# Spreading VectorE's row statistics over the block groups, and ending the DMA transposes two groups early

## The chip, the cores and the metric

The kernel runs on one core of one Trainium2 chip. The metric is device time in microseconds (us) of one execution.

## The reference, cut to what matters

```python
x = A_x                                              # 2048 tokens x 1024, bf16
x = x + _A_ref(_layernorm(x), A_w_r, A_w_i)          # spectral filter: rfft2, times W, irfft2
x = x + _B_ref(_layernorm(x), B_w1, B_b1, B_w2)      # dense 1024 -> 3584, mish, dense 3584 -> 1024
x = x + _A_ref(_layernorm(x), A_w_r, A_w_i)
x = x + _B_ref(_layernorm(x), B_w1, B_b1, B_w2)
```

The change concerns the two dense layers `_B_ref` with their layer normalisation; the same program text makes both. "First layer" and "second layer" below mean these two.

## The kernel before

Tokens are held as 16 tiles of 128, four to a chunk. A dense layer multiplies chunks 0 and 1 with the first weights, the last eight of its fourteen weight blocks as *block groups* (`quads`); then come 16 half-tile products with the second weights for these chunks (`mm2`, "the second product"); then the same for chunks 2 and 3, there with all fourteen blocks as groups. While chunks 0 and 1 are multiplied, tiles 8 to 15 must be normalised by VectorE and transposed by DMAs for their own turn. That work hangs on the groups through the function `after`.

A block group saves a product by working with sums of weight blocks and sums of tokens. Its seven products of four matmuls land in three PSUM banks (PSUM, `PS` in the profile's rows, holds the results of the matmuls), and VectorE's five additions (`add`) tie them together:

```python
for n in range(N + 1):
    if n < N:
        product(n, a, "A11", "B11", True); ...copy by ScalarE...
        product(n, b, "S2", "T2", True);   add(u2, b, p1)
    if n:                                   # the group before is finished here
        product(n - 1, pb, "A22", "T4", False); add(q1, pb, q1); ...
        product(n - 1, pd, "S4", "B22", False); add(q2, pd, q2); ...
        after(n - 1)                        # <- statistics, roots, normalisations, transposes
    if n < N:
        ...three more products...
        add(u3, b, p1); add(u3, d, u3)      # the next A22 and S4 add to these banks
```

VectorE runs its program in order, so whatever `after` puts in delays the two `u3` additions, and TensorE (PE) waits for these before its next `A22`.

```python
def stats_half(self, j, h): ... bn_stats ...        # stats_dve(j): two of these and a bn_aggr
def scales(self, j0, n):                            # the "root chain": 1/sqrt by 8 tiny steps for n tiles
    on(tensor_scalar ...); on(tensor_scalar ... int32 ...)
    for _ in range(2):
        on(tensor_tensor(a, r, r, mult)); on(tensor_tensor(a, a, h, mult)); on(scalar_tensor_tensor ...)
def apply(self, j, out=False): ... tensor_scalar(b, XS[j], mean, r, subtract, mult)   # the normalisation
def turned(c, t, xn): ... eight closures, each one SyncE DMA with transpose=True, appended to `turning`
def turn(n): ... pops n of them into SyncE's program
def normal(j): ... apply(j), then turned(...)
def residual(j): ... XS[j] += spectral part, by VectorE
def token_sums(p, last): ... three, then one more, subtractions of transposed tiles for the next groups
```

SyncE also issues the loads of the second weights (`load_w2`). The second product begins with 20 matmuls on weight blocks loaded earlier; the first two blocks (`load_w2(0, 0)` and `(0, 1)`) share memory with the slot of the last group and can be loaded only when PE has finished that group. In the first layer GpSimd forms the weight sums (`fill_slot`: one addition and three subtractions for each of the groups' blocks, called its subtractions below) beside all this and keeps them in DRAM; in the second layer they are only loaded.

## Time and profile before

| | before |
|---|---|
| time, median of the first 3 runs | 1009.95 us (1009.22 to 1011.17) |
| span of the profiled run | 1006.9 us |
| busy: PE, VectorE, ScalarE, GpSimd | 92%, 51%, 38%, 16% |
| first layer: eight groups, then 16 second products | 59.66 us, 104.76 us |
| second layer: the same | 53.31 us, 99.85 us |
| all the rest | 689.32 us |

The stretches are read from PE's rows in order of time: from the first matmul of the groups to the first of the second product, and from there to the next block product. At PE's pace the groups need 48.4 us and the 448 matmuls of a second product 96.8 us; what a stretch has beyond that is waiting or a slow clock. The lines that carry this stand in the prediction.

In the lines of the profile, L1188 are the groups' matmuls, L1193 their additions, L1241 the matmuls of the second product, L1253 its additions, L1164 the token sums, L1084 GpSimd's subtractions, L499 to L512 the root chain, L521 the normalisation, L250 and L251 the DMAs; x84 means 84 instructions merged into one row. A granted clock of 1.00 is PE's full speed.

### The profile page before, as it was taken

What the parts mean: (1) busy time and instruction counts of PE and PEld (TensorE: products, weight loads), DVE (VectorE), ACT (ScalarE), POOL (GpSimd) and SP (SyncE); (2) the same over time, 40 slices, a digit from 0 to 9 for tenths busy, and PEclk for the clock granted to TensorE, in tenths of its full rate; (3) what the DMA queues carried; (4) which work ended last, traced back from release to release, by engine and by line L of the source; (5) the groups of instructions that cost most, each with busy time, mean ns of one, the idle gap of its engine ahead of it and who ended that gap; (6) DMA issues with size and microseconds to landing.
All of it is one profiled execution on the core that took longest, in us unless ns stands there. A gap on an engine that the chain in (4) does not pass through costs nothing. (4 is left out here: it accounts for less than half of the span.)

```text
span 1006.9 us, 13694 instructions
## 1 busy us (share of the span) xinstructions
PE 928.8 (92%) x5650; PEld 490.6 (49%) x5650; DVE 513.1 (51%) x947; ACT 377.9 (38%) x531; POOL 158.7 (16%) x184
## 2 busy tenths in 40 slices
PE   0899699897999999999998987998899999999998
PEld 0677475343444444444447756743344444444443
DVE  6697567785227655525326855748611325551111
ACT  7798484352000255500008966644400015550000
POOL 3831007910600050000621200000000000000000
PEclk9999899898999999999999997999999999999999
DMA  9969844545611164220941885344281114421000
GB/s 276 274 202 324 204 117 149 211 145 178 212 34 50 53 225 146 95 89 32 225 98 43 236 219 147 147 146 123 88 249 22 58 37 161 164 94 63 32 32 21
DMA packets 140431, 136.48 MB, mean 136 GB/s; under 512 B 74368, under 2 KB 121296, under 8 KB 140368
## 3 DMA queue, kind: packets, MB, share of 16 engines
q1 hardware_dynamic: 127264, 95.26, 31.9%
q0 software_dynamic: 10928, 38.69, 11.8%
q10 hardware_dynamic: 2176, 1.66, 0.5%
q8 instruction: 44, 0.72, 0.3%
q14 instruction: 19, 0.16, 0.0%
HBM read 97.49 MB, written 33.55 MB: 130 GB/s over the span
## 5 line engine op out<-in xcount | busy, mean ns | idle before, releaser
L1241 PE MATMUL PS<-ARENA 128*128 128x512 bf16 x1792 | 389.9, 380 | 8.7 <-DMA ARENA<-in_B_w_dram 8.7
L1188 PE MATMUL PS<-ARENA 128*128 128x512 f16 (+1 forms) x1232 | 271.7, 382 | 14.6 <-DVE ARENA L1193 14.1
L1241 PEld LDWEIGHTS PS<-ARENA 128*128 128x128 bf16 x1792 | 175.6, 98 | 222.6 <-issue 12.6
L1188 PEld LDWEIGHTS PS<-ARENA 128*128 128x128 bf16 x1232 | 120.0, 98 | 165.7 <-DVE ARENA L1193 21.6
L1193 DVE TENSOR_TENSOR ARENA<-PS,ARENA 128x512 f32<-128x512 f32 x220 | 151.1, 691 | 93.9 <-PE PS L1188 91.9
L1253 DVE TENSOR_TENSOR XS<-PS,XS 128x512 bf16<-128x512 f32 x63 | 43.6, 692 | 276.2 <-PE PS L1241 276.2
L577 ACT ACTIVATE ARENA<-PS 128x512 f32<-128x512 f32 (+2 forms) x66 | 51.8, 784 | 257.3 <-PE PS L1188 246.9
L1198 ACT ACTIVATE ARENA<-ARENA,B 128x512 bf16<-128x512 f32 x132 | 95.2, 722 | 73.3 <-DVE ARENA L1193 67.7
L1084 POOL TENSOR_TENSOR ARENA<-ARENA 128x512 bf16<-128x512 bf16 x56 | 68.3, 1219 | 124.6 <-DVE ARENA L521 59.3
L1149 PE MATMUL PS<-ARENA 128*128 128x256 bf16 (+1 forms) x576 | 87.5, 310 | 0.3
L1149 PEld LDWEIGHTS PS<-ARENA 128*128 128x128 bf16 x576 | 55.8, 99 | 27.1 <-DVE ARENA L1115 1.0
L469 DVE BATCH_NORM_STATS2 BN<-XS 128x6 f32<-128x512 bf16 x99 | 64.2, 678 | 6.2 <-DMA XS<-in_A_x_dram 5.2
L1153 ACT ACTIVATE ARENA<-PS,B 128x256 bf16<-128x256 f32 (+1 forms) x72 | 38.4, 542 | 36.0 <-PE PS L1149 35.4
L1198 ACT ACTIVATE ARENA<-PS,B 128x512 bf16<-128x512 f32 x44 | 30.3, 688 | 20.4 <-PE PS L1188 20.4
L441 ACT ACTIVATE RS<-MV,EPS 128x2 f32<-128x2 f32 (+2 forms) x5 | 1.5, 297 | 95.6 <-DVE MV L472 83.7
L802 PE MATMUL PS<-ARENA 128*128 128x256 bf16 x256 | 32.4, 273 | 3.9 <-DVE ARENA L791 3.2
L780 ACT ACTIVATE ARENA<-PS 128x1024 bf16<-128x1024 f32 x32 | 33.3, 1071 | 4.5 <-PE PS L776 4.5
L728 PE MATMUL PS<-FD,ARENA 128*128 128x256 bf16 (+1 forms) x256 | 31.8, 271 | 2.9 <-DVE ARENA L995 1.6
L784 DVE TENSOR_TENSOR ARENA<-ARENA 128x1024 bf16<-128x1024 bf16 x32 | 22.0, 688 | 20.9 <-ACT ARENA L780 15.3
L1164 DVE TENSOR_TENSOR ARENA<-ARENA 128x2048 f16<-128x2048 bf16 x16 | 22.7, 1417 | 17.7 <-PE PS L1149 17.3
L813 ACT ACTIVATE ARENA<-PS 128x1024 bf16<-128x1024 f32 x28 | 29.9, 1090 | 3.8 <-PE PS L802 3.8
L1023 PE MATMUL PS<-MT,ARENA 128*128 128x32 bf16 (+1 forms) x512 | 21.5, 201 | 10.2 <-DMA ARENA<-u_scratch 6.8
(95 smaller groups left out, 705.3 us busy)
## 6 DMA issues: line engine op xcount, KB each, us to landing
ARENA<-in_B_w_dram SPq DMA_DIRECT2D x62, 512.0 KB, 5.8
ARENA<-w1s_scratch SPq DMA_DIRECT2D x30, 896.0 KB, 4.6
w1s_scratch<-ARENA POOLq DMA_DIRECT2D x14, 896.0 KB, 4.0
u_scratch<-ARENA SPq DMA_DIRECT2D x14, 512.0 KB, 3.8
ARENA<-u_scratch SPq DMA_DIRECT2D x14, 512.0 KB, 5.8
w_scratch<-ARENA POOLq DMA_DIRECT2D x8, 512.0 KB, 7.2
ARENA<-w_scratch POOLq DMA_DIRECT2D x8, 512.0 KB, 5.3
out_dram<-XS SPq DMA_DIRECT2D x16, 256.0 KB, 2.0
```

The lines of the kernel that those rows point to most:

```text
L469: self.op(self.dve, lambda e: e.bn_stats(self.BN[:, j, 6 * h:6 * h + 6], self.XS[:, j, 512 * h:512 * h + 512]), reads=[self.r_xs[j]], part ...
L577: fn = (lambda e: e.activation(dst, src, ACT.Copy)) if scale is None else \
L780: self.op(act, lambda e: e.activation(x.ap.rearrange("p a b -> p (a b)"), ps, ACT.Copy, scale=SIG), reads=banks, writes=[x.res])
L802: fns.append(lambda e, c=c, part=part: e.matmul(ps[:, c * 256:(c + 1) * 256], yk.ap[:, part, c * P:(c + 1) * P], t[:, (128, 0)[part]:(384, ...
L1084: self.op(self.pool, lambda e, dst=A(dst), x=A(x), y=A(y), op=op: e.tensor_tensor(dst, x, y, op), reads=[b.res] + list(after), writes=[b.rs])
L1149: fns.append(lambda e, db=db, bank=bank, fl=fl: e.matmul(PS[:, bank, 0:w], wb.ap[:, db, fl * P:(fl + 1) * P], x.ap[:, db, tok], start=(db ...
L1153: self.op(act, lambda e, bank=bank, ft=ft: e.activation(at.ap[:, ft, tok], PS[:, bank, 0:w], ACT.Mish, bias=self.B1[:, ft:ft + 1]), reads= ...
L1188: self.group([lambda e, db=db: e.matmul(PS[:, bank, :], A[:, db, :], mov[:, db, :], start=(start and db == 0), stop=(db == 3), skip_group_ ...
L1193: self.op(dve, lambda e: e.tensor_tensor(dst.ap, PS[:, bank, :], x.ap, ALU.add), reads=[self.r_bank[bank], x.res], writes=[dst.res])
L1198: self.op(act, lambda e: e.activation(at.ap[:, ft, :], src, ACT.Mish, bias=self.B1[:, ft:ft + 1]), reads=[res, self.r_b1], writes=[ra])
L1241: fns.append(lambda e, ft=ft, w=W2[h][ft // 4]: e.matmul(PS[:, bank, :], at.ap[:, ft, t * P:(t + 1) * P], w.ap[:, ft % 4, :], start=(ft == ...
L1253: self.op(dve, lambda e: e.tensor_tensor(xs, PS[:, bank, :], xs, ALU.add), reads=[self.r_bank[bank]], writes=[self.r_xs[j]])
```

## The change

The intent: at most one statistic or one root chain of two tiles in a block group, beside at most one normalisation, so that VectorE comes back in time for its additions; and no transposes in SyncE's queue in the last two groups, so that the weight loads go out at once. What no longer fits goes into the loop of the second product.

```diff
--- before.py
+++ after.py
@@ -1390,18 +1390,17 @@
             if 1 <= n < 4:
                 for i in ((2,), (3, 4), (5, 6))[n - 1]:
                     load_w2(0, i)
-            for j in ((8, 9), (), (10,), (11,), (), (12,), (13,), ())[n]:
+            for j in ((8,), (9,), (), (10,), (11,), (), (), ())[n]:
                 self.stats_dve(j)
-            if n == 0:
-                self.scales(8, 2)
-            if n == 3:
-                self.scales(10, 2)
-            if 1 <= n < 5:
-                normal(7 + n)
-            if n in (2, 3):
-                for j in range(8 + 2 * n, 10 + 2 * n):
+            if n in (2, 5):
+                self.scales(8 + 2 * (n // 4), 2)
+            if n in (2, 3, 5, 6):
+                normal((0, 0, 8, 9, 0, 10, 11)[n])
+            if n > 5:
+                for j in range(2 * n, 2 * n + 2):
                     residual(j)
-            turn(4)
+            if n < 6:
+                turn(4)
         quads(list(range(6, 14)), order, B, after)
         for i in range(2):
             load_w2(0, i)
@@ -1413,14 +1412,18 @@
         self.xn_buf = [self.alloc(f"XN{i}", self.ob["TS"] + i * 2048, [self.D]) for i in range(4)]
         for n in range(16):
             if n == 0:
+                self.stats_dve(12)
+                self.stats_dve(13)
+                self.scales(12, 2)
+            if n == 1:
                 self.stats_dve(14)
                 self.stats_dve(15)
-                self.scales(12, 4)
+                self.scales(14, 2)
             if n < 4:
                 normal(12 + n)
             t = n % 8
             mm2(t // 4, t % 4, n // 8)
-            turn(4)
+            turn(5)
             if n == 10:
                 token_sums(1, last=False)
                 B = token_sums(1)
```

## The prediction

> **What bounds the kernel now.** The page gives the frame: TensorE (PE) is busy 92% of the span and ends the chain, so the change can gain only what PE waits. I read PE's waits next, longest first.
>
> ```profile
> PE PS L598 <- DVE ARENA L595: 21.8, 1, 21.8
> PE PS L1188 <- DVE ARENA L1193: 14.1, 9, 4.9
> PE PS L1241 <- DMA ARENA<-in_B_w_dram: 8.7, 2, 5.7
> ```
>
> The columns are total us, times, longest. The first is in the prologue, which the diff leaves alone. The second is PE in the first dense product (block products, L1188) waiting for VectorE's additions; the third is PE at the start of the second product (L1241) waiting for weights. The changed code runs in both dense layers, so I read PE in order of time there, the first layer above, the second below.
>
> ```profile
> 174.38 12.25 PE L1188 MATMUL PS<-ARENA 128*128 128x512 bf16 x56
> 191.54 21.52 PE L1188 MATMUL PS<-ARENA 128*128 128x512 f16 x84 [4.91 <-DVE ARENA L1193]
> 214.94 16.58 PE L1188 MATMUL PS<-ARENA 128*128 128x512 f16 x76 [1.88 <-DVE ARENA L1193]
> 232.31 1.90 PE L1188 MATMUL PS<-ARENA 128*128 128x512 f16 x8 [0.79 <-DVE ARENA L1193]
> 234.04 4.48 PE L1241 MATMUL PS<-ARENA 128*128 128x512 bf16 x20
> 244.25 18.10 PE L1241 MATMUL PS<-ARENA 128*128 128x512 bf16 x73 [5.72 <-DMA ARENA<-in_B_w_dram]
> ...
> 681.57 18.60 PE L1188 MATMUL PS<-ARENA 128*128 128x512 f16 x84 [1.49 <-DVE ARENA L1193]
> 702.03 16.58 PE L1188 MATMUL PS<-ARENA 128*128 128x512 f16 x76 [1.87 <-DVE ARENA L1193]
> 728.61 6.63 PE L1241 MATMUL PS<-ARENA 128*128 128x512 bf16 x30 [3.00 <-DMA ARENA<-in_B_w_dram]
> ```
>
> A matmul costs 0.216 us at pace (428 in 92.54 us in the chain). The 224 of the eight block groups are 48.4 us, but take 59.66 (174.38 to 234.04) and 53.31 us (667.82 to 721.13). In the second layer the waits explain the excess: 1.49, 1.87, a 0.61 hidden in the first row, and 0.79 after the last group. In the first layer 4.91 + 0.61 + 1.88 + 0.79 leave 3.1 us over. The windows show why: the granted clock was 0.50 from 191.5 to 196 and again from 244.2 to 248. After the 5.72 us wait the slow clock cost another 2.3 us (94.72 against 92.54 us for the same 428 matmuls); after the 3.00 us wait it cost nothing.
>
> **VectorE.** Each group is 28 matmuls, 6.05 us, and carries five additions of 0.69 us. The diff's work sits between the third and fourth. In the second layer after group 0 that work lasts 4.42 us (676.40 to 680.82) and PE waits 1.49; after group 3, 4.80 us and 1.87. So about 2.9 us are free.
>
> **SyncE's queue** in the second layer:
>
> ```profile
> 708.02 15.26 SPq L250 DMA_TRANSPOSE ARENA<-ARENA  x12
> 723.32 9.52 SPq L251 DMA_DIRECT2D ARENA<-in_B_w_dram  x9
> ```
>
> A transpose takes the queue 1.27 us. PE begins L1241 at 721.13, when the buffer for the first two weight blocks is free, yet their loads are issued only at 723.32, behind transposes; in the first layer 238.85 against 234.04. The blocks land 5.3 us after the first issue, while PE has other weights for only 4.48 us.
>
> **What the skill says.** "TensorE: Matmul & The Clock Gate", What's actually happening: the clock halves after an idle window of about 3.4 us, free-running, and returns after a busy one. The trace agrees: 4.91 and 5.72 us of idling are followed by a 0.50 clock, 3.00 is not. "SBUF — State Buffer", SBUF: two separate sides: VectorE operations in a two-port mode or with two SBUF inputs share an exclusive port pair with GpSimd, and the loser waits for the whole instruction. The trace agrees: while GpSimd's 1.15 us subtractions (L1084) ran, root steps that normally take 0.16 us took 1.60 and 1.00; the same chain, 1.57 us in the second layer, took 4.98. Statistics (0.64 us) did not slow. "DMA: Bandwidth & Descriptors", Issuing engines are not separate DMA queues: all DMAs run on the same 16 engines and interleave. The trace agrees that traffic matters: transposes take 1.43 us each (32 in 45.64) in the first layer, beside loads, and 1.27 (12 in 15.27) later.
>
> **The change part by part.**
>
> *Second layer, groups.* One statistic of a whole row is 1.45 us, a root chain 1.6, a normalisation 0.54, two residual additions 1.29. Before, the groups carry 4.4, 0.5, 3.2, 4.8, 0.5, 1.5, 1.5 us. After, 1.5, 1.5, 2.2, 2.0, 1.5, 2.2, 1.8: all under 2.9. Saved: 1.49 + 0.61 + 1.87 = 4.0 us. The 0.79 stays; in the last group there is nothing for PE to do meanwhile.
>
> *First layer, groups.* The same three waits and the slow clock go: 4.91 + 3.1 + 0.61 + 1.88 = 10.5. But GpSimd works until 203.6, and the moved root chain now starts near 195.1 (two groups after 183.0), still beside it. Laying the chain against GpSimd's instruction ends, two small steps per 1.2 us, plus the normalisation gives 5.4 us, 2.5 over the free 2.9. Net 8.0.
>
> *Weight loads.* No transpose stands in front any more. The loads go out about 0.2 us after PE's last block product and land some 5.1 later, against 4.48 of covered work: a wait of about 0.8 in the second layer (3.00 before), saved 2.2. In the first, the transposes end barely in time: wait 1.0 instead of 5.72, and no slow clock: 4.7 + 2.3 = 7.0.
>
> *Given back.* Before, 28 of 32 transposes are issued in the groups; after, 16. So 48, not 36, follow the weight loads. The five per block of the loop set only their place in the program; SyncE issues as fast as its queue goes. The first layer needs 15.5 us for twelve loads, 50.75 for 36 transposes and 12 x 1.27 = 15.2 for the extra ones, and 2.3 to land: 83.8 us after the first load. The token sums, which need them all, then take 5.0 us of VectorE, and the next addition 0.69: about 89.8 us after PE starts L1241. Before:
>
> ```profile
> 238.85 15.47 SPq L251 DMA_DIRECT2D ARENA<-in_B_w_dram  x12
> 254.37 45.64 SPq L250 DMA_TRANSPOSE ARENA<-ARENA  x32
> ...
> 289.85 15.27 SPq L250 DMA_TRANSPOSE ARENA<-ARENA  x12
> ...
> 312.22 5.00 DVE L1164 TENSOR_TENSOR ARENA<-ARENA 128x2048 f16<-128x2048 bf16 x4
> ```
>
> There they ended at 305.1, seven us before the sums. PE has three banks, so it can go on three tiles past the sums, and must have that addition when tile 14 starts: 1.0 + 14 x 6.05 = 85.7 us. Wait: about 4.1 us. VectorE's backlog (3.4 us a tile) costs 0.6 more at the next block product, and a slow clock after 4.1 us has perhaps one chance in four of 3 us: 0.8. Lost: 5.5. In the second layer the loads take 12.1 us and the transposes 1.29 each; the sums end some 82 us after the start and tile 14 begins at 85.7: no wait, 2.8 us to spare.
>
> Sum: first layer 8.0 + 7.0 - 5.5 = 9.5; second 4.0 + 2.2 = 6.2; together 15.7. PE sets the end after both, so it passes through: 1009.95 - 15.7 = 994.3 us, 1.6% faster.
>
> **Rivals.** (1) *No new wait from the transposes.* If the 48 run a few us faster than laid out, all of it stays: about 21 us, 989 us. For: the second layer's queue is faster (12.1 us for its loads). Against: the first layer's pace is measured, and twelve more at the lowest steady pace are 15 us, twice the slack of seven. (2) *The late transposes bind harder.* If SyncE's queue is slower beside the loads, the wait grows past 5 us, the clock halves, the second layer may wait too: 5 to 8 us lost more, 1000 us. For: 1.43 us each in the first layer. (3) *GpSimd's lock takes the place of the wait.* The moved root chain could lose 4 us or more at group 2 and halve the clock: back to 1000. For: the chain took 5 us beside GpSimd before. Against: statistics do not suffer and one of the two is gone from that group. (4) *Weight latency.* If two loads need 5.3 us whatever is before them, the waits are 1.0 to 1.2; a difference of 0.5.
>
> **Range and chances.** The uncertain terms are the transposes' wait (0 to 7), the lock (1 to 4), the clock (0 to 3 each) and the weight waits (0.5 to 1.5). Together they give about ±5: 990 to 1000. Faster by 2% means under 989.75 us, which needs rival 1 nearly whole: 0.13. Slower by 2% would need a new wait of 35 us: 0.01.
>
> **What would show it.** Right: no 4.91 us wait in the first layer's groups, but one of 1 to 4 us two groups later, with root steps of about 1 us beside GpSimd; no waits in the second layer's groups but 0.79; weight waits near 1 us, their loads issued within a us of PE's first L1241 matmul; in the first layer token sums that start some 16 us after their tile's matmuls end, transposes ending just before, and a PE wait on VectorE of about 4 us before tile 14; in the second layer none there. It is wrong if the transposes end in time (then near 989), if SyncE's loads still start late, or if the clock shows 0.50 anywhere in these stretches.

## The result, and the profile after

The changed kernel takes 995.53 us (median of 4 runs, 994.99 to 998.02), the kernel before 1010.56 us (4 runs). The ratio is 0.9851 with a 95% interval of 0.9821 to 0.9881. Ratios here are the mean time of one kernel's fast runs over that of the other's of the same rounds, so not quite the ratio of the medians quoted. It is 1.5% faster.

PE's waits in the changed kernel (total us, times, longest); the lines answer to the three at the head of the prediction:

```profile
PE PS L598 <- DVE ARENA L595: 22.4, 1, 22.4
PE PS L1188 <- DVE ARENA L1193: 7.2, 6, 3.3
...
PE PS L1241 <- DVE XS L1253: 3.8, 1, 3.8
...
PE PS L1241 <- DMA ARENA<-in_B_w_dram: 1.9, 2, 1.0
```

The waits on VectorE in the block products fell from 14.1 to 7.2 us, those on weight loads from 8.7 to 1.9. One line is new: a wait of the second product on VectorE, 3.8 us. In order of time on PE (start, duration, instruction, in brackets the idle time before it and what ended it), the first layer, then the second:

```profile
174.56 24.34 PE L1188 MATMUL PS<-ARENA 128*128 128x512 bf16 x110
202.23 22.62 PE L1188 MATMUL PS<-ARENA 128*128 128x512 f16 x102 [3.33 <-DVE ARENA L1193]
225.64 1.90 PE L1188 MATMUL PS<-ARENA 128*128 128x512 f16 x8 [0.79 <-DVE ARENA L1193]
227.38 4.48 PE L1241 MATMUL PS<-ARENA 128*128 128x512 bf16 x20
232.77 80.45 PE L1241 MATMUL PS<-ARENA 128*128 128x512 bf16 x364 [0.91 <-DMA ARENA<-in_B_w_dram]
316.98 13.63 PE L1241 MATMUL PS<-ARENA 128*128 128x512 bf16 x55 [3.76 <-DVE XS L1253]
...
660.36 46.78 PE L1188 MATMUL PS<-ARENA 128*128 128x512 bf16 x212
707.93 1.90 PE L1188 MATMUL PS<-ARENA 128*128 128x512 f16 x8 [0.79 <-DVE ARENA L1193]
709.67 4.48 PE L1241 MATMUL PS<-ARENA 128*128 128x512 bf16 x20
715.15 92.54 PE L1241 MATMUL PS<-ARENA 128*128 128x512 bf16 x419 [0.99 <-DMA ARENA<-in_B_w_dram]
```

(Some matmul records are missing, hence 419 where there are 428.) The second layer's groups run as one row: no wait but the 0.79 at the end. The first layer keeps one wait, 3.33 us, two groups later than the 4.91 it replaces. VectorE in that group:

```profile
195.23 0.36 DVE L499 TENSOR_SCALAR RS<-MV 128x2 f32<-128x2 f32 x1
195.62 0.17 DVE L501 TENSOR_SCALAR RS<-RS 128x2 int32<-128x2 int32 x1
195.83 1.00 DVE L510 TENSOR_TENSOR RS<-RS 128x2 f32<-128x2 f32 x1
196.86 0.16 DVE L511 TENSOR_TENSOR RS<-RS 128x2 f32<-128x2 f32 x1
197.05 1.00 DVE L512 SCALAR_TENSOR_TENSOR RS<-RS 128x2 f32<-128x2 f32 x1
198.09 0.16 DVE L510 TENSOR_TENSOR RS<-RS 128x2 f32<-128x2 f32 x1
198.28 0.16 DVE L511 TENSOR_TENSOR RS<-RS 128x2 f32<-128x2 f32 x1
198.48 1.62 DVE L512 SCALAR_TENSOR_TENSOR RS<-RS 128x2 f32<-128x2 f32 x1
200.13 1.45 DVE L521 TENSOR_SCALAR FD<-XS,MV,RS 128x1024 bf16<-128x1024 bf16 x1
```

Steps on two elements per partition last 0.16 to 0.36 us or 1.00 to 1.62, and the normalisation 1.45 instead of 0.54. The whole takes 6.35 us where about 2.9 are free, and PE waits 3.33. Then SyncE's queue in the first layer, and after it VectorE at the token sums:

```profile
227.57 15.81 SPq L251 DMA_DIRECT2D ARENA<-in_B_w_dram  x12
243.42 66.58 SPq L250 DMA_TRANSPOSE ARENA<-ARENA  x48
```

```profile
311.31 5.01 DVE L1164 TENSOR_TENSOR ARENA<-ARENA 128x2048 f16<-128x2048 bf16 x4 [12.67 <-DMA ARENA<-ARENA]
316.24 0.68 DVE L1253 TENSOR_TENSOR XS<-PS,XS 128x512 bf16<-128x512 f32 x1
```

The loads go out 0.19 us after PE's first matmul of the second product (before: 4.8 us after). But 48 transposes follow, and they end at 310.0. VectorE stood for 12.67 us in front of the token sums, and PE got its addition only then. The windows show a granted clock of 0.50 from 317 to 319 after that wait.

By stretches: 59.66 became 52.82 and 104.76 became 103.07 us in the first layer; 53.31 became 49.31 and 99.85 became 97.85 in the second. That is 6.8 + 1.7 + 4.0 + 2.0 = 14.5 us gained. The rest of the span, which the diff does not touch, went from 689.32 to 690.15.

### The profile page after: what moved, and what is told of

Same layout as the page of the kernel before. It is cut to its first block, busy times and chain, and to the rows that moved or that the text cites. A ratio compares the mean times of both kernels' runs of the same rounds, so it can differ in the third digit from the quotient of the medians.

```text
span 993.2 us, 13632 instructions
## 1 busy us (share of the span) xinstructions
PE 918.4 (92%) x5572; PEld 488.5 (49%) x5650; DVE 517.3 (52%) x963; ACT 377.8 (38%) x531; POOL 158.2 (16%) x184
## 5 line engine op out<-in xcount | busy, mean ns | idle before, releaser
L1241 PE MATMUL PS<-ARENA 128*128 128x512 bf16 x1756 | 387.4, 380 | 7.6 <-DVE XS L1253 3.8
L1241 PEld LDWEIGHTS PS<-ARENA 128*128 128x128 bf16 x1792 | 175.3, 98 | 219.2 <-issue 4.7
L1188 PE MATMUL PS<-ARENA 128*128 128x512 f16 (+1 forms) x1210 | 267.0, 379 | 8.9 <-DVE ARENA L1193 7.2
L1188 PEld LDWEIGHTS PS<-ARENA 128*128 128x128 bf16 x1232 | 119.8, 98 | 155.4 <-DVE ARENA L1193 11.4
L784 DVE TENSOR_TENSOR ARENA<-ARENA 128x1024 bf16<-128x1024 bf16 x32 | 22.0, 688 | 20.2 <-ACT ARENA L780 14.5
```

What stands on the lines that cost most here:

```text
L1188: self.group([lambda e, db=db: e.matmul(PS[:, bank, :], A[:, db, :], mov[:, db, :], start=(start and db == 0), stop=(db == 3), skip_group_ ...
L1241: fns.append(lambda e, ft=ft, w=W2[h][ft // 4]: e.matmul(PS[:, bank, :], at.ap[:, ft, t * P:(t + 1) * P], w.ap[:, ft % 4, :], start=(ft == ...
```

## The experiments

Seven kernels were run, all with correct results but the one marked. Stretches of all of them, in us (the last column is the span less the four):

| kernel | median us | 1st groups | 1st second product | 2nd groups | 2nd second product | rest |
|---|---|---|---|---|---|---|
| before | 1009.87 (8 runs) | 59.66 | 104.76 | 53.31 | 99.85 | 689.3 |
| changed | 995.53 | 52.82 | 103.07 | 49.31 | 97.85 | 690.2 |
| changed, again | 995.83 | 54.54 | 104.56 | 49.31 | 97.75 | 687.3 |
| VectorE's order only | 1006.34 | 54.50 | 105.22 | 49.30 | 107.44 | 687.8 |
| transposes only | 1000.06 | 59.53 | 97.65 | 53.32 | 97.70 | 691.3 |
| sums after tile 12 | 988.86 | 54.51 | 97.79 | 49.31 | 97.65 | 687.5 |
| GpSimd quiet (wrong result) | 987.34 (1 run) | 49.30 | 98.39 | 49.31 | 97.92 | 690.6 |
| chain later | 986.34 | 50.39 | 98.11 | 49.30 | 97.75 | 688.3 |
| chain later, two tiles first | 984.91 | 50.35 | 96.69 | 49.31 | 96.69 | 689.0 |

"Rest" moves by up to 4 us between kernels that share its text, and by 2.8 between two traces of the same changed kernel. Up to 1.7 us of this is PE's first wait in the prologue (L598), 20.7 to 22.4 us in these traces. So totals decide only larger questions; the stretches and the waits in them decide the smaller ones.

### VectorE's order alone

The changed kernel, with transposes in every group again:

```diff
-            if n < 6:
-                turn(4)
+            turn(4)
...
-            turn(5)
+            turn(4)
```

> The changed order of VectorE's work, but four transposes issued after every block group as in the kernel before, the last two groups too. My theory (two coupled parts): the group waits are those of the changed kernel (3.3 us in the first layer, only 0.79 in the second), but the normalisations come later, so the transposes run past the end of the groups and the first weight loads start about 8 us (first layer) and 6 us (second) after PE's first L1241 matmul; PE then waits about 9 and 6.5 us for them, with a slow clock after each (2 to 3 us). Total about 1009 us, no faster than before. Rival (the parts add up, each worth its own waits): 995.5 plus the weight waits of before (about 5 us more), near 1001 us.

Measured: 1006.34 us, ratio to before 0.9965 (0.9936 to 0.9995). The groups gained as in the changed kernel, but the second product lost it again. PE in the second layer, in order of time, and SyncE's queue there:

```profile
711.12 4.48 PE L1241 MATMUL PS<-ARENA 128*128 128x512 bf16 x20
723.28 95.45 PE L1241 MATMUL PS<-ARENA 128*128 128x512 bf16 x428 [7.67 <-DMA ARENA<-in_B_w_dram]
```

```profile
707.06 10.16 SPq L250 DMA_TRANSPOSE ARENA<-ARENA  x8
717.27 9.18 SPq L251 DMA_DIRECT2D ARENA<-in_B_w_dram  x9
```

The loads go out 6.2 us after PE's first matmul, behind eight transposes, and PE waits 7.67 us (6.80 in the first layer), then runs at half clock for a while (95.45 for what takes 92.54). Expected were 6.5 in the second layer and 9 in the first, and 1009 us in all, 2.7 more than measured: the four stretches together are 1.1 us under those of before, the rest 1.5. So the two parts do not add: spreading the normalisations pushes the transposes back onto the weight loads, and only ending the transposes early makes it pay. The rival, 1001, falls.

### The transposes alone

The kernel before, with no transposes in the last two groups:

```diff
-            turn(4)
+            if n < 6:
+                turn(4)
...
-            turn(4)
+            turn(5)
```

> VectorE's order of the kernel before, but no transposes issued in the last two groups. My theory: the group waits stay as before (4.9, 0.6, 1.9 and the slow clock in the first layer; 1.5, 0.6, 1.9 in the second), the weight loads start at once and PE waits about 1 us for them in each layer instead of 5.7 and 3.0; 44 transposes follow the loads and just end in time, no wait at the token sums. Saves about 7 + 2 = 9 us: about 1001.5. Rival (the weight wait is the loads' own latency, not their place in the queue): the waits stay near 3 to 6 us and the time near 1009.

Measured: 1000.06 us, ratio 0.9894 (0.9870 to 0.9917). PE at the start of the second product, first layer and second:

```profile
239.56 92.54 PE L1241 MATMUL PS<-ARENA 128*128 128x512 bf16 x428 [0.79 <-DMA ARENA<-in_B_w_dram]
...
721.28 92.54 PE L1241 MATMUL PS<-ARENA 128*128 128x512 bf16 x428 [0.85 <-DMA ARENA<-in_B_w_dram]
```

The group waits are those of before (4.91, 1.88, 1.49, 1.88 in PE's rows), the weight waits are 0.79 and 0.85, and the second products take 97.65 and 97.70 us. That is 7.1 and 2.2 us less. So all but these 0.8 us of the wait was the loads' place in the queue, not their latency. The 44 transposes here cost no wait at the token sums: there is no such wait in PE's list.

### The token sums two tiles later

The changed kernel, with one number edited:

```diff
-            if n == 10:
+            if n == 12:
                 token_sums(1, last=False)
```

> The changed kernel with the token sums put two tiles later in VectorE's program (after tile 12 instead of 10). My theory (the sums stand in VectorE's queue waiting for the last transposes, and PE for the additions behind them): the 3.8 us wait of PE in the first layer goes, nothing else changes: about 991.5 us. Rival (the sums are needed that early, or PE then waits at the next block product instead): the wait moves there, time within 1 us of 995.5.

Measured: 988.86 us, ratio to before 0.9781 (0.9760 to 0.9801), against 0.9851 for the change; the interval spans the 2% line, so by the rule this is "unclear". The 48 transposes still end at 309.3 and the sums start at 310.6, but the additions of tiles 11 and 12 now stand before them. PE's row of the first layer's second product has no wait on VectorE and no slow clock:

```profile
232.13 92.54 PE L1241 MATMUL PS<-ARENA 128*128 128x512 bf16 x428 [0.94 <-DMA ARENA<-in_B_w_dram]
...
328.88 11.40 PE L1188 MATMUL PS<-ARENA 128*128 128x512 f16 x52 [0.76 <-DVE ARENA L1193]
```

The stretch is 97.79 us against 103.07, 5.3 us less: 3.8 of wait and 1.5 of slow clock. The wait did not move to the next block product, which waits 0.76 as before. The expectation had 4 us of gain; I had left the clock out of it. The median fell by 6.7.

### The changed kernel again

> The changed kernel once more, unaltered, for a comparison in the same rounds as the next kernels: moving the token sums gained 6.7 us by the medians where the wait and the slow clock after it account for 5.3 in the trace; the traces also differ by 2.4 us in the prologue, which no edit touches. If that is chance of the run, this kernel gives 993 to 996 and its prologue moves too; if it belongs to the kernel, its block products begin near 174.5 us again and 172 is peculiar to the other.

Measured: 995.83 us, ratio 0.9857 (0.9830 to 0.9883), in the rounds of the next kernels. Its block products begin at 172.42 us, where the first trace had 174.56. So that difference is chance. Its trace is otherwise worse: after a group wait of 3.38 us the clock was at 0.50 from 202 to 204 and the groups took 54.54 us; the wait at the token sums was 5.18 us. The four stretches together are 306.2 us, against 299.3 with the later sums: 6.9 us, the difference of the medians. By the second product alone the late transposes cost 5.3 us in the first trace and 6.8 in this one, where SyncE's queue of loads and transposes took 1.5 us longer.

### GpSimd quiet in the group with the root chain

Wrong (relative error 0.033): in the kernel with the later sums, GpSimd writes zeros for the last three weight blocks of the first layer instead of subtracting.

```diff
-            self.op(self.pool, lambda e, ...: e.tensor_tensor(dst, x, y, op), reads=[b.res] + list(after),
+            fn = (lambda e, ...: e.memset(dst, 0.0)) if fg > 10 else \
+                (lambda e, ...: e.tensor_tensor(dst, x, y, op))
+            self.op(self.pool, fn, reads=[b.res] + list(after),
```

> Wrong result on purpose: the kernel with the token sums after tile 12, but in the first layer GpSimd fills the sums of the last three weight groups with zeros instead of subtracting, so it is quiet when the first root chain runs in group 2. Lock theory: the chain takes 1.6 us as in the second layer, its steps 0.16 us each, and PE's 3.3 us wait in the first layer's groups is gone entirely (only 0.79 left). Rival (chain and normalisation too long, or something else of the first layer such as the transfers slows VectorE): the wait stays at 2 to 3 us.

Measured: one look, 987.34 us, state unknown. The first layer's groups take 49.30 us, as in the second layer, and the 3.3 us wait is gone. The chain on VectorE:

```profile
195.25 0.16 DVE L499 TENSOR_SCALAR RS<-MV 128x2 f32<-128x2 f32 x1
195.44 0.51 DVE L501 TENSOR_SCALAR RS<-RS 128x2 int32<-128x2 int32 x1
195.99 0.16 DVE L510 TENSOR_TENSOR RS<-RS 128x2 f32<-128x2 f32 x1
...
197.16 0.55 DVE L521 TENSOR_SCALAR FD<-XS,MV,RS 128x1024 bf16<-128x1024 bf16 x1
```

One step was held for 0.35 us beside the last zero-fill; the others take 0.16, the normalisation 0.55. The DMAs of this kernel are the same, though GpSimd issues its own some us earlier; one of them (at 196.23) starts in the middle of the chain and slows no step. So the slow steps were GpSimd's subtractions, and the rival falls.

### The chain one group later

The changed kernel with the first root chain moved behind most of GpSimd's work, and the sums after tile 13 to keep the later transposes harmless:

```diff
-            for j in ((8,), (9,), (), (10,), (11,), (), (), ())[n]:
+            for j in ((8,), (9,), (10,), (), (11,), (), (), ())[n]:
-            if n in (2, 5):
+            if n in (3, 5):
                 self.scales(8 + 2 * (n // 4), 2)
-            if n in (2, 3, 5, 6):
-                normal((0, 0, 8, 9, 0, 10, 11)[n])
+            if n in (3, 4, 5, 6):
+                normal(5 + n)
...
-            turn(5)
-            if n == 10:
+            turn(6)
+            if n == 13:
```

> The changed kernel with the first root chain and normalisation one group later (exchanged with a statistic), where GpSimd stops about 3 us into the chain, and the token sums after tile 13 so that the later transposes cost nothing. Lock theory: the 3.3 us wait in the first layer's groups becomes about 1.1 us, as only the first steps of the chain meet GpSimd; about 2.2 us less than the run with the sums after tile 12, near 989.5 us. Rival (the chain with a normalisation is too long for a group by itself): 3.3 us again, one group later, and a time like the run with the sums after tile 12.

Measured: 986.34 us, ratio 0.9760 (0.9737 to 0.9784). The wait in the first layer's groups is 0.91 us; two steps of the chain took over 1 us (1.13 and 1.00) before GpSimd stopped, the rest 0.16. The groups take 50.39 us. It is faster than before. By the medians it is 2.5 us faster than the kernel with the later sums, and the four times of each, taken in the same rounds, do not overlap (985.63 to 986.93 against 987.57 to 989.12), though the intervals of the two ratios do. In the trace the groups gained 4.1 us: 2.4 of wait, and the slow clock that had followed it.

### Two tiles before the late weights

The kernel above, with the first 20 matmuls of tile 1 put in front of the eight of tile 0 that need the late weight blocks:

```diff
...                                    # mm2 gets a fourth argument: which part to do
-            mm2(t // 4, t % 4, n // 8)
+            if n == 0:
+                mm2(0, 0, 0, 0)        # tile 0, the 20 matmuls on early weights only
+                mm2(0, 1, 0, 0)        # tile 1, the same, into the next bank
+            mm2(t // 4, t % 4, n // 8, 1 if n < 2 else None)    # 1: only the last eight
```

> The kernel with the later chain, but the second product starts with 20 matmuls each of two tiles before the eight that need the late weight blocks: 8.9 us of cover instead of 4.5. Theory (what is left of the weight wait is transfer time, about 5.3 us, less the cover): the waits of 1.25 and 0.9 us go, about 2 us less, 984.3 us. Rival (the first two tiles' work shifts the wait elsewhere, to VectorE's additions or the token sums): no gain, 986.3.

Measured: 984.91 us (983.83 to 987.87), ratio 0.9754 (0.9726 to 0.9781). No wait on the weight loads is left in PE's list, and the second products run as single rows of all 448 matmuls (L1243 is L1241 of the other kernels, moved by the edit):

```profile
224.26 96.86 PE L1243 MATMUL PS<-ARENA 128*128 128x512 bf16 x448
...
699.61 96.86 PE L1243 MATMUL PS<-ARENA 128*128 128x512 bf16 x448
```

Both stretches are 96.69 us, 1.4 and 1.1 less. About 0.4 comes back at the next block product of the first layer, whose wait on VectorE grew from 0.76 to 1.12. The gain of 1.4 us in the medians is within their scatter, so the rows show it, not the times. This kernel beats both: 2.5% under before by its ratio, where the change alone is 1.4 to 1.5% under.

## Why the prediction was right

It said 994.3 us, in a range of 990 to 1000; measured were 995.53 and, repeated, 995.83. Its steps, by its own numbers:

- **Second layer, groups:** 4.0 us predicted, 4.0 measured (53.31 to 49.31). The group's free time of 2.9 us was the right reading.
- **First layer, groups:** 8.0 predicted, 6.8 in the first trace and 5.1 in the repetition. The mechanism, GpSimd's lock, was right and is shown by the quiet kernel. The size was off: the wait was 3.33 us, not 2.5. The term mis-sized is the pair of chain and normalisation, laid at 5.4 us and measured at 6.35: the eight steps took 4.87 us, as laid out, but the normalisation, charged with its undisturbed 0.54, took 1.45. Nor had I charged a slow clock after this wait: in the repetition and in two other kernels a wait of 3.3 to 3.4 us cost another 1.7 us, in the first trace nothing.
- **Weight loads:** waits of 1.0 and 0.8 predicted, 0.91 and 0.99 measured, with no slow clock. Saved in the second layer: 2.2 predicted, 2.0 measured. In the first layer the transposes-only kernel, which has no wait at the token sums, saved 7.1 where 7.0 were predicted. (The 2.3 us of slow clock in that sum are 2.2 by the rows shown: 94.72 less 92.54.) The transposes-only kernel shows the cause.
- **Given back in the first layer:** addition for tile 14 ready 89.8 us after PE's start predicted; PE resumed at 89.6 (316.98 less 227.38). Wait 4.1 predicted, 3.76 measured. The clock was charged with 0.8 as a chance of one in four; it came in both traces and cost about 1.5 us. The backlog of 0.6 did not come: the next block product waits 0.76, as before. In sum 5.5 predicted and 5.3 lost (6.8 in the repetition, where the wait was 5.18).
- **Second layer, token sums:** no wait, 2.8 us to spare predicted. The sums stood waiting there too (9.1 us), but ended at 792.3, the addition at about 792.9, and tile 14 begins at about 795.4 (709.67 + 0.99 + 14 x 6.05): 2.4 us to spare.
- **Sum:** 15.7 predicted, 14.5 in the four stretches of the first trace and 11.4 in the repetition, whose median is nearly the same because its rest was 2.0 us shorter than that of before. So that the total comes within 1.5 us is in part luck: the scatter of the rest is larger than that.

Rival 1 (no wait from the transposes) was wrong for the change but right as the gain to be had: moving the sums gave it. Rival 2 named 5 us of wait and a halved clock in the first layer: the clock halved in both traces, the wait passed 5 us in the repetition alone, and the second layer did not wait. Rival 3, the lock, was true in part: 3.3 us of wait instead of 4, and a halved clock in the repetition. Rival 4 cannot be told apart: the weight waits, 0.90 to 0.99 us in the two traces, lie between both accounts. Of the prediction's own signs of being wrong one came true: the clock shows 0.50 in these stretches, from 317 to 319. It stood beside a charge of 0.8 us for just that, so the prediction contradicted itself there; the sum had it, if too small. What the prediction did not see is how strongly the two halves of the diff depend on each other: VectorE's order alone is worth 0.35% by its ratio, the transposes alone 1.06%, both 1.5%.

Open: why the rest of the span differs by up to 4 us between kernels that share its text, and why the clock halves after some waits of 3.3 us and not after others. The free-running window of the Trainium skill's "TensorE: Matmul & The Clock Gate", What's actually happening, would explain the latter, but no run here shows the window itself.

## What to carry to other kernels

Work given to an engine between two of its critical operations has a budget that the trace shows (busy time less wait); spread it so that no step exceeds it, and count with the slower durations that a neighbour's lock causes. When work is moved out of the way, follow what it triggers: here later normalisations meant later transposes, these met first the weight loads and then the token sums. An in-order engine that waits for a late transfer holds everything behind it, so put that wait as late as its consumer allows; here one edited number was worth nearly half as much as the whole change.

## What the Trainium skill lacked or had wrong

- "SBUF — State Buffer", Who interferes with whom, states the lock, and the runs agree. It lacks what a chain of tiny operations pays: each blocked step ends with the neighbour's running instruction (1.00 us of its 1.22), and one step slips through at the seam to the next. Eight steps of 0.16 us and a normalisation of 0.54 took 6.35 us beside subtractions of about 1.2 us.
- The same section warns of GpSimd's DMA issue being held up by VectorE. The other direction has no number there: a two-input step that began inside GpSimd's 0.56 us issue of a DMA ended only with the first subtraction after it, 1.62 us in all. The issue alone does not hold such a step: in the quiet kernel and in the one with the later chain, two steps each began inside an issue that no subtraction followed, and took 0.16 us. Why the step waits for a subtraction that has not begun stays open.
- "TensorE: Matmul & The Clock Gate", What's actually happening, gives an idle window of about 3.4 us. Here the clock halved after waits of 3.33, 3.34 and 3.38 us and did not after another of 3.33 and one of 3.00: a margin below 3.4 is wise. In the stretches of the table one halving cost about 1.4 to 3.1 us.
- "DMA: Bandwidth & Descriptors", DMA Transpose (X-bar), has no time for a transpose of 128x128 bf16 within SBUF as its issuing queue sees it (elsewhere the page has a bandwidth and sequencer cycles of other cases): 1.27 us each here in a quiet stretch, 1.39 on average (48 in 66.58 us) behind and beside weight loads, 2.3 us to land.
